# Attention matmuls of a fused attention and two-MLP kernel, planned as undivided blocks with the two array halves alternating

## The chip, the cores and the metric

The kernel runs on one core of a Trainium2 chip. The metric is device microseconds of one execution, and the time before is the median of three runs. A profiled execution, with its own time, gives the trace.

## What is computed

A block-recurrent attention with decay (2 batches, 8 heads, 768 positions, head size 64), whose output, transposed to 1536 tokens of width 512, goes through two MLPs, all in float32.

```python
def _attn_ref(q, k, v, lam):            # block = 64, nb = 12
    for b in range(nb):
        intra = np.einsum('bhic,bhjc->bhij', qb, kb) * Dmask[None]
        intra = np.einsum('bhij,bhjd->bhid', intra, vb)
        inter = np.einsum('bhid,bhde->bhie', qb * lam_pow[None], kv_state)
        out[:, :, sl] = intra + inter
        kv_state = lam_block[None, :, None, None] * kv_state + np.einsum('bhsd,bhse->bhde', kb_dec, vb)

def _moe_ref(x, w_gate, w_val, w_out):  # 512 -> 1536 -> 512
    return sigmoid(x @ w_gate) * (x @ w_val) @ w_out

def _moe2_ref(x, w_in, w_out):          # 512 -> 2048 -> 512
    return elu(x @ w_in) @ w_out
```

## The kernel before, in words

**Attention.** The 768 positions are taken in six chunks of 128 (the loop over `c`, line 562). For each chunk and each of the two batches `b` there are up to four sorts of TensorE work, each a group of small float32 matmuls: `st` (line 558), scores, eight per chunk and batch, four head pairs `p` times two halves `q`; its operands lie in 64 partitions, so it uses the upper or the lower half of the array's rows, and it writes one PSUM bank per half (`A1`, `B1`). `x` (line 595), scores times values, eight per chunk and batch, all 128 rows and 64 columns, where the column half is `q`. `x` again (line 600), state times query, from the second chunk on, 64 rows and 64 columns. `u` (line 579), the update of the state, sixteen per chunk, five chunks, 128 rows and 64 columns. In the trace each of these float32 matmuls is two MATMUL instructions, so eight matmuls are x16.

Between them stand VectorE's masking of the scores (`pr`, line 559), ScalarE's decayed keys (`kd`, line 569), GpSimd's decayed queries (`ql`, line 573), the state (`sn`) and `split_chunk` (line 420), which copies a finished chunk out of PSUM and splits it into a high and a low part for the MLPs.

**MLPs.** The products (`product`, line 451) are fp32r matmuls of 256 or 512 columns, three per term (high by high, high by low, low by high), on seven products a Strassen-like scheme; `unit` (line 650) does the output matmuls into `xu`. During the attention, the first MLP's products G and V for token part 0 follow chunk 1, for part 1 chunk 3 and for part 2 chunk 5 (lines 614 to 617). The name `warm` in the trace is PSUM bank A0: 24 bf16 matmuls at the start (line 543), and later the bank of the products.

**What sets the order.** The kernel's code only records operations (`Work.record`, line 160). `hazards` (line 179) works out what must precede what; `issue` (line 286) runs five rounds of a list scheduler (`run`, line 235), in which each engine takes, among its ready operations, the one with the highest priority from the backward run, and emits all instructions in the order of the best plan. Each engine then works in that order on the chip. The plan's times come from `cost` (line 135). A float32 matmul of n columns holds TensorE `n / 1.2 + 20` ns there, whatever stood before it. Every matmul is an operation of its own and may be planned anywhere between others. ScalarE's function tables (sigmoid, then exp) have an order among them (line 229) and no cost.

Of the kernel before, what the change touches and what calls it, by code (L numbers as in the profile page):

```python
# [3 lines left out]

# [1 line left out]

# [5 lines left out]
F32 = mybir.dt.float32  # L12
# [4 lines left out]
ALU = mybir.AluOpType  # L17
PSUM = bass.MemoryType.PSUM

P = 128  # L20
B, H, S, D = 2, 8, 768, 64
NP = H // 2
CH = 128
# [85 lines left out]


class Op:
    __slots__ = ("eng", "call", "reads", "writes", "gap", "took", "port", "table", "preds")


class Engine:
# [8 lines left out]

class Work:
    MATMUL = {512: (229, 391), 384: (173, 335), 256: (120, 283)}
    HANDOFF = {"tensor": 60, "vector": 35, "scalar": 35, "gpsimd": 78, "sync": 30}
    OVERLAP = {"vector": 83, "scalar": 101, "gpsimd": 45}

    def __init__(self, nc):  # L130
        self.nc, self.ops = nc, []
        for name in ENGINES:
            setattr(self, name, Engine(self, name))

    def cost(self, op, fn, args, kw):
        outs, ins = op.writes, [v for v in op.reads if v.ix.size > 1]
        n = (outs or op.reads)[0].ix.size
        on_chip = [v for v in ins if not v.buf.psum]
        op.port = False
        if op.eng == "tensor":  # L140
            dt = args[-1].dtype if len(args) > 2 else kw["rhs"].dtype
            if dt == F32R:
                return self.MATMUL[n]
            if dt == BF16:
                return n / 2.4 + 3, n / 2.4 + 170
            return n / 1.2 + 20, n / 0.6 + 210
        if op.eng == "sync":
            return 60, n * P * 4 / 400
        if op.eng == "gpsimd":
            op.port = len(on_chip) > 1  # L150
            took = 180 + 2.18 * n
        elif op.eng == "vector":
            single = len(ins) == 1 and len(on_chip) == 1 and not outs[0].buf.psum
            op.port = len(on_chip) > 1 or single
            took = 150 + 0.53 * n if single else 130 + 1.07 * n
        else:
            took = (190 if on_chip else 160) + 0.84 * n + (93 if len(op.reads) > 1 else 0)
        return took - self.OVERLAP[op.eng], took

    def record(self, eng, fn, args, kw):  # L160
        op = Op()
        op.eng = eng
        out, *rest = (kw[x] for x in ("out", *(x for x in kw if x != "out"))) if "out" in kw else (*args, *kw.values())
        op.writes = [out] if isinstance(out, View) else []
        op.reads = [v for v in rest if isinstance(v, View)]
        for v in op.reads + op.writes:
            assert v.turn >= v.buf.turn, "a tile is used behind its successor"
            v.buf.turn = v.turn
        op.gap, op.took = self.cost(op, fn, args, kw)
        func = kw.get("func", args[2] if fn == "activation" and len(args) > 2 else None)  # L170
        op.table = {AF.Sigmoid: 1, AF.Exp: 2}.get(func, 0)
        real = lambda v: v.ap() if isinstance(v, View) else v

        def call():
            return getattr(getattr(self.nc, eng), fn)(*(real(a) for a in args), **{k: real(a) for k, a in kw.items()})  # L175
        op.call = call
        self.ops.append(op)

    def hazards(self):
# [55 lines left out]
    def run(self, preds, key, backward=False):  # L235
        ops = self.ops[::-1] if backward else self.ops
        n = len(ops)
        after, left = [[] for _ in range(n)], [len(p) for p in preds]
        for k, p in enumerate(preds):
            for x in p:  # L240
                after[x].append(k)
        ripe, soon = {e: [] for e in ENGINES}, {e: [] for e in ENGINES}
        at, start, end = [0.0] * n, [0.0] * n, [0.0] * n
        free = dict.fromkeys(ENGINES, 0.0)
        port = queue = 0.0
        for k in range(n):
            if not left[k]:
                heapq.heappush(soon[ops[k].eng], (0.0, k))
        for _ in range(sum(op.eng is not None for op in ops)):
            t, e = min((free[e] if ripe[e] else max(free[e], soon[e][0][0]), i, e)  # L250
                       for i, e in enumerate(ENGINES) if ripe[e] or soon[e])[::2]
            while soon[e] and soon[e][0][0] <= t:
                k = heapq.heappop(soon[e])[1]
                heapq.heappush(ripe[e], (key[k], k))
            k = heapq.heappop(ripe[e])[1]
            op = ops[k]
            if e == "sync":
                queue = max(t + 1400, queue) + op.took
                free[e], end[k] = t + op.gap, queue + 300
            elif e == "tensor":  # L260
                t += 60 if t > free[e] + 1 else 0
                free[e], end[k] = t + op.gap, t + op.took
            else:
                go = max(t, port) if op.port else t
                if op.port:
                    port = go + op.gap
                free[e], end[k] = go + op.gap, go + op.took
            start[k] = t
            done = [k]
            while done:  # L270
                x = done.pop()
                for s in after[x]:
                    f = ops[s].eng
                    ready = free[e] if f == e == "tensor" and x == k else end[x] + self.HANDOFF.get(f, 0)
                    at[s] = max(at[s], ready)
                    left[s] -= 1
                    if left[s]:
                        continue
                    if f is None:
                        start[s] = end[s] = at[s]  # L280
                        done.append(s)
                    else:
                        heapq.heappush(soon[f], (at[s], s))
        return start, end
# [32 lines left out]
def tile_decay_attention_two_mlps(  # L317
# [13 lines left out]
    nc = work = Work(tc.nc)  # L331
    sb = Arena(ctx.enter_context(tc.tile_pool(name="sb", bufs=1)))
    ps = Arena(ctx.enter_context(tc.tile_pool(name="ps", bufs=1, space=PSUM)), psum=True)
# [202 lines left out]
    n = 1  # L536
# [14 lines left out]
    def scores(c):  # L551
        prs[c] = []
        for b in range(2):
            pr = sb.tile([P, 2, NP, CH], F32, f"woh_{b}", name="pr")
            for q, r in ((0, lo), (1, hi)):
                st = ps.tile([P, NP, CH], F32, ("A1", "B1")[q], name="st")
                for p in range(NP):
                    nc.tensor.matmul(st[:, p], lhsT=tin[c][r, b, 0, p], rhs=tin[c][r, b, 1, p], start=True, stop=True)
                nc.vector.tensor_tensor(out=pr[:, q], in0=st, in1=da[:, q], op=ALU.mult)
            prs[c].append(pr)  # L560

    for c in range(NCH):
# [10 lines left out]
                nc.gpsimd.tensor_tensor(out=ql[:, b], in0=tin[c][:, b, 1], in1=lp, op=ALU.mult)  # L573
        if more:
            u = ps.tile([P, 2, NP, D], F32, "C1", name="u")
            for b in range(2):
                for p in range(NP):
                    for q, r in ((0, lo), (1, hi)):
                        nc.tensor.matmul(u[r, b, p], lhsT=kd[:, b, 2 * p + q], rhs=nat_of[c][:, b, 1, 2 * p + q],
                                         start=True, stop=True)  # L580
            sn = sns[c + 1] = sb.tile([P, 2, NP, D], F32, f"wt1_{c % 2}", name="sn")
            if c == 0:
                nc.vector.tensor_copy(sn, u)
            else:
                for p in range(NP):
                    nc.vector.scalar_tensor_tensor(out=sn[:, :, p], in0=sns[c][:, :, p], scalar=l_ch[:, p],
                                                   in1=u[:, :, p], op0=ALU.mult, op1=ALU.add)
        xa = sb.tile([P, 6, CH], F32, "wol_1", name="xa")
        later = []
        parts = None  # L590
        for b in range(2):
            x = ps.tile([P, NP, CH], F32, f"xu_{b}", name="x")
            for p in range(NP):
                for q, r in ((0, lo), (1, hi)):
                    nc.tensor.matmul(x[r, p], lhsT=nat_of[c][:, b, 1, 2 * p + q], rhs=prs[c][b][:, q, p],
                                     start=p == 0 or not c, stop=not c, skip_group_check=True)
            if c:
                for p in range(NP):
                    for r in (lo, hi):
                        nc.tensor.matmul(x[r, p], lhsT=sns[c][r, b, p], rhs=ql[r, b, p], start=False, stop=True,  # L600
                                         skip_group_check=True)
            if b == 0:
                parts = split_chunk(xops[s], slice(t0, t0 + CH), x, later, xa)
            else:
                later.append(x)
            next(parts)
# [211 lines left out]
```

## Time and profile before

| what | value |
|---|---|
| median of three runs | 621.32 us (620.34 to 622.68) |
| the profiled execution, its own time | 623.05 us |
| its span, first to last instruction | 621.3 us |
| mean granted TensorE clock | 0.999 |
| TensorE (PE) busy | 609.7 us, 98% |
| VectorE (DVE) / ScalarE (ACT) / GpSimd (POOL) busy | 398.7 / 301.1 / 327.0 us |

The profile counts an instruction as busy from its start to its modelled end. TensorE's matmuls overlap, so what one costs is read from its start to the next one's start.

### The profile page before, as it was taken

Reading aid. Unit: us, or ns where it says so; the run is one execution under the profiler, and the core shown is the slowest. Engines: PE = TensorE matmul, PEld = TensorE weight load, DVE = VectorE, ACT = ScalarE, POOL = GpSimd, SP = SyncE. Lnnn points to the kernel's source line nnn. Section 1 sums busy time; section 2 is a strip of 40 time slices with the busy share of each in tenths; the row PEclk is TensorE's granted clock in tenths of the full one; section 3 lists DMA queues with packets and bytes.
Section 4 is the critical chain, followed back from the end, with each engine's and each line's share of the span. In section 5 each row is a group of like instructions: output and inputs, shape, how many; then the busy total and the mean of one; then the engine's idle time right before and its main releaser. Section 6 shows DMA issues by size and latency. Waiting matters only on the chain.

```text
span 621.3 us, 9271 instructions
## 1 busy us (share of the span) xinstructions
PE 609.7 (98%) x3632; PEld 516.3 (83%) x3632; DVE 398.7 (64%) x684; ACT 301.1 (48%) x571; POOL 327.0 (53%) x264
## 2 busy tenths in 40 slices
PE   9999999999899999999999899999999999999997
PEld 5778888988788888888899788888788888888886
DVE  5657646536855755755755988485757776776474
ACT  3655234665324425424414788783728282844160
POOL 2458435858747737737624897447546364551100
PEclk9999999999999999999999999999999999999999
DMA  8913110233032111111110110311311211200005
GB/s 323 418 74 136 69 69 7 77 122 134 8 130 69 69 68 69 69 68 69 69 68 2 69 69 0 136 70 68 137 68 69 69 69 69 68 1 1 0 18 186
DMA packets 8828, 51.98 MB, mean 84 GB/s; under 512 B 1104, under 2 KB 1360, under 8 KB 3024
## 3 DMA queue, kind: packets, MB, share of 16 engines
q1 hardware_dynamic: 8784, 51.39, 22.3%
q8 instruction: 28, 0.46, 0.3%
q14 instruction: 16, 0.13, 0.1%
HBM read 48.24 MB, written 3.15 MB: 83 GB/s over the span
## 4 chain that ended last, share of the span: by engine, by line
PE 85%; DVE 5%; ACT 4%; DMA 3%; issue 2%; POOL 2%; ACTq 0%; SPq 0%; DVEq 0%; POOLq 0%
PE xu L175 32%; PE B L175 17%; PE warm L175 10%; PE A L175 9%; PE C L175 6%; PE x L175 5%; PE st L175 4%; DVE w L175 2%; DMA w<-in_w_in 2%; ACT w L175 1%; PE u L175 1%; DMA w<-in_w_gate 1%; POOL t L175 1%; ACT gh L175 1%; DVE xu L175 0%
## 5 line engine op out<-in xcount | busy, mean ns | idle before, releaser
L175 PE MATMUL xu<-gh,woh 128*128 128x512 f32 (+1 forms) x322 | 126.5, 396 | 4.9 <-DVE acc L175 2.5
L175 PE MATMUL xu<-gl,woh 128*128 128x512 f32 (+1 forms) x322 | 125.3, 390 | 0.0
L175 PE MATMUL xu<-gh,wol 128*128 128x512 f32 (+1 forms) x322 | 124.9, 389 | 0.0
L175 DVE TENSOR_TENSOR acc<-xu,acc 128x512 f32<-128x512 f32 x120 | 81.5, 688 | 49.6 <-PE xu L175 49.0
L175 POOL TENSOR_TENSOR gl<-sig,gh 128x1024 fp32r<-128x1024 f32 (+1 forms) x38 | 81.4, 2154 | 44.3 <-ACT gh L175 43.3
L175 POOL TENSOR_TENSOR t<-w 128x256 f32<-128x256 f32 (+1 forms) x80 | 69.0, 891 | 49.1 <-DVE w L175 45.0
L175 POOL TENSOR_TENSOR l<-t,h 128x768 fp32r<-128x768 f32 (+1 forms) x38 | 64.1, 1692 | 35.2 <-ACT h L175 32.6
L175 PEld LDWEIGHTS xu<-gh,woh 128*128 128x128 f32 x322 | 60.5, 188 | 19.6 <-issue 3.4
L175 PEld LDWEIGHTS xu<-gh,wol 128*128 128x128 f32 x322 | 60.5, 188 | 12.1
L175 PEld LDWEIGHTS xu<-gl,woh 128*128 128x128 f32 x322 | 60.6, 188 | 10.0
L175 POOL TENSOR_TENSOR wol<-w,woh 128x512 fp32r<-128x512 f32 x26 | 33.2, 1294 | 63.7 <-ACT woh L175 57.4
L175 ACT CAST gh<-sig 128x512 fp32r<-128x512 f32 (+1 forms) x58 | 45.0, 784 | 25.0 <-DVE sig L175 22.9
L175 ACT ACTIVATE w<-w 128x1024 f32<-128x1024 f32 x34 | 38.7, 1137 | 29.3 <-POOL wol L175 14.9
L175 DVE SCALAR_TENSOR_TENSOR w<-w,w 128x1024 uint32<-128x1024 uint32 x34 | 50.6, 1489 | 0.2
L175 DVE TENSOR_SCALAR w<-w 128x1024 uint32<-128x1024 uint32 x34 | 35.0, 1030 | 24.1 <-ACT w L175 23.8
L175 ACT ACTIVATE sig<-B 128x256 f32<-128x256 f32 (+1 forms) x62 | 28.4, 458 | 38.3 <-PE B L175 34.0
L175 DVE TENSOR_TENSOR wt<-B,wt 128x256 f32<-128x256 f32 (+1 forms) x45 | 22.9, 508 | 28.9 <-PE B L175 26.0
L175 ACT CAST h<-t 128x512 fp32r<-128x512 f32 (+1 forms) x40 | 29.1, 727 | 14.9 <-POOL t L175 8.4
L175 ACT ACTIVATE sig<-sig 128x256 f32<-128x256 f32 (+1 forms) x68 | 34.2, 507 | 1.4
L175 ACT ACTIVATE sig<-warm 128x256 f32<-128x256 f32 x36 | 13.8, 383 | 40.9 <-PE warm L175 21.8
L175 ACT CAST woh<-w 128x1024 fp32r<-128x1024 f32 x14 | 14.8, 1054 | 38.5 <-PE xu L175 27.8
L175 POOL TENSOR_TENSOR ql<-tin,low 128x512 f32<-128x512 f32 x10 | 13.5, 1362 | 35.1 <-PE x L175 22.4
(143 smaller groups left out, 1558.0 us busy)
## 6 DMA issues: line engine op xcount, KB each, us to landing
w<-in_w_out SPq DMA_DIRECT2D x14, 1024.0 KB, 4.8
w<-in_w_in SPq DMA_DIRECT2D x8, 1024.0 KB, 4.8
nat<-in_att SPq DMA_DIRECT2D x6, 1024.0 KB, 10.1
w<-in_w_gate SPq DMA_DIRECT2D x6, 1024.0 KB, 4.9
w<-in_w_val SPq DMA_DIRECT2D x6, 1024.0 KB, 4.8
tin<-in_att SPq DMA_DIRECT2D x5, 1024.0 KB, 10.5
out_t<-o SPq DMA_DIRECT2D x11, 256.0 KB, 2.0
tin<-in_att SPq DMA_DIRECT2D x2, 512.0 KB, 6.2
```

What stands on the lines that cost most here:

```text
L175: return getattr(getattr(self.nc, eng), fn)(*(real(a) for a in args), **{k: real(a) for k, a in kw.items()})
```

## The change

Every run of attention matmuls that belongs together (one `st`, one `u`, one of each kind of `x`) is recorded inside `with nc.together()`, which joins them into one operation of the plan, never divided, whose reads and writes are those of all its parts. In `scores` the loop order changes: per head pair first the lower, then the upper half, into both banks, then the two VectorE multiplications. The plan's cost of a float32 matmul becomes `n / 2.4 + 2.5` ns held and `n / 1.2 + 165` ns to its end. TensorE operations get a `shape`, and the plan adds 150 ns where the shape differs from that of the operation before. The plan adds 1283 ns where ScalarE's table changes. No instruction's operands, size or number changes, nor do buffers or DMAs.

```diff
+    SWITCH, TABLE = 150, 1283
...
         if op.eng == "tensor":
-            dt = args[-1].dtype if len(args) > 2 else kw["rhs"].dtype
+            dt = kw["rhs"].dtype
+            op.shape = dt if dt != F32 else (kw["lhsT"].halves, kw["lhsT"].ix.size) if len(kw["rhs"].halves) < 2 else kw["lhsT"].ix.size
...
-            return n / 1.2 + 20, n / 0.6 + 210
+            return n / 2.4 + 2.5, n / 1.2 + 165
...
+    @contextmanager
+    def together(self):
+        self.block = []
+        yield
+        parts, self.block = self.block, None
+        op = parts[0]
+        calls = [x.call for x in parts]
+        op.took = sum(x.gap for x in parts) + parts[-1].took - parts[-1].gap
+        op.gap = sum(x.gap for x in parts)
+        op.reads = [v for x in parts for v in x.reads]
+        op.writes = [v for x in parts for v in x.writes]
+        op.call = lambda: [c() for c in calls][-1]
         self.ops.append(op)
...
             elif e == "tensor":
                 t += 60 if t > free[e] + 1 else 0
+                t += self.SWITCH if op.shape != shape else 0
+                shape = op.shape
                 free[e], end[k] = t + op.gap, t + op.took
             else:
+                if op.table and op.table != table:
+                    t, table = t + self.TABLE, op.table
...
-            for q, r in ((0, lo), (1, hi)):
-                st = ps.tile([P, NP, CH], F32, ("A1", "B1")[q], name="st")
+            sts = [ps.tile([P, NP, CH], F32, bank, name="st") for bank in ("A1", "B1")]
+            with nc.together():
                 for p in range(NP):
-                    nc.tensor.matmul(st[:, p], lhsT=tin[c][r, b, 0, p], rhs=tin[c][r, b, 1, p], start=True, stop=True)
-                nc.vector.tensor_tensor(out=pr[:, q], in0=st, in1=da[:, q], op=ALU.mult)
+                    for st, r in zip(sts, (lo, hi)):
+                        nc.tensor.matmul(st[:, p], lhsT=tin[c][r, b, 0, p], rhs=tin[c][r, b, 1, p], start=True, stop=True)
+            for q in range(2):
+                nc.vector.tensor_tensor(out=pr[:, q], in0=sts[q], in1=da[:, q], op=ALU.mult)
...
+            with nc.together():
+                for b in range(2):
+                    for p in range(NP):
+                        for q, r in ((0, lo), (1, hi)):
+                            nc.tensor.matmul(u[r, b, p], lhsT=kd[:, b, 2 * p + q],
+                                             rhs=nat_of[c][:, b, 1, 2 * p + q], start=True, stop=True)
...
```

The two groups of `x` (lines 593 and 598) get the same `with` around their loops, whose order stays (head pair, then half).

## Rows read from the trace of the kernel before

**Rows 1.** The page: busy time, and the chain that ended last by engine.
```profile
PE 609.7 (98%) x3632; PEld 516.3 (83%) x3632; DVE 398.7 (64%) x684; ACT 301.1 (48%) x571; POOL 327.0 (53%) x264
...
PE 85%; DVE 5%; ACT 4%; DMA 3%; issue 2%; POOL 2%; ACTq 0%; SPq 0%; DVEq 0%; POOLq 0%
```

**Rows 2.** Busy time of each engine by stretch (us, instructions), clock, DMA share, GB/s.
```profile
10.00:20.00 10.00, 9.96 (x116) 8.09 (x113) 7.03 (x13) 6.62 (x18) 4.60 (x4) 1.00 1.02 424
...
30.00:40.00 10.00, 10.00 (x89) 8.05 (x85) 7.48 (x15) 6.94 (x16) 7.50 (x5) 1.00 0.38 156
...
6.00:29.00 23.00, 22.96 (x238) 17.68 (x237) 12.93 (x25) 11.78 (x33) 9.31 (x8) 1.00 1.02 422
29.00:100.00 71.00, 71.00 (x648) 58.58 (x646) 42.03 (x87) 29.82 (x68) 34.06 (x25) 1.00 0.23 88
100.00:182.00 82.00, 79.02 (x444) 68.38 (x443) 50.23 (x71) 39.70 (x69) 58.32 (x50) 1.00 0.24 90
...
340.00:400.00 60.00, 56.82 (x334) 49.62 (x333) 47.71 (x104) 48.63 (x107) 45.09 (x37) 1.00 0.15 54
```

**Rows 3.** Waits from 6 to 100 us: engine waiting, for whom, us, times, longest.
```profile
ACT xa L175 <- PE x L175: 27.5, 8, 9.2
POOL ql L175 <- PE x L175: 22.4, 3, 8.1
DVE pr L175 <- PE st L175: 14.5, 11, 3.4
```

**Rows 4.** TensorE's groups from 6.1 to 99.6 us: count, busy us, mean ns, idle.
```profile
L175 PE MATMUL st<-tin 64*128 64x128 f32 x192 | 26.3, 288 | 0.0
L175 PE MATMUL x<-pr,nat 128*64 128x128 f32 x192 | 21.3, 282 | 0.0
L175 PE MATMUL x<-ql,sn 64*64 64x128 f32 x160 | 15.8, 278 | 0.0
L175 PE MATMUL u<-nat,kd 128*64 128x64 f32 x160 | 9.3, 228 | 0.0
...
L175 PE MATMUL warm<-x11h,h 128*128 128x256 f32 x8 | 2.6, 322 | 0.0
```

**Rows 5.** TensorE in order of time, last chunk: start us, us, group, count.
```profile
92.35 1.09 PE L175 MATMUL x<-pr,nat 128*64 128x128 f32 x8
93.36 1.16 PE L175 MATMUL st<-tin 64*128 64x128 f32 x8
94.45 1.08 PE L175 MATMUL x<-ql,sn 64*64 64x128 f32 x8
95.46 1.09 PE L175 MATMUL x<-pr,nat 128*64 128x128 f32 x8
96.48 1.08 PE L175 MATMUL x<-ql,sn 64*64 64x128 f32 x8
97.50 1.09 PE L175 MATMUL x<-pr,nat 128*64 128x128 f32 x16
98.52 1.09 PE L175 MATMUL x<-ql,sn 64*64 64x128 f32 x16
99.54 0.39 PE L175 MATMUL B<-xPh,h 128*128 128x256 f32 x1
...
99.88 0.28 PE L175 MATMUL B<-xPh,l 128*128 128x256 f32 x1
100.00 0.28 PE L175 MATMUL B<-xPh,h 128*128 128x256 f32 x1
```

**Rows 6.** TensorE in order of time, elsewhere in the attention.
```profile
6.04 1.71 PE L175 MATMUL st<-tin 64*128 64x128 f32 x16
7.68 1.90 PE L175 MATMUL warm<-idle 128*128 128x512 bf16 x8
...
29.11 1.71 PE L175 MATMUL st<-tin 64*128 64x128 f32 x16
...
49.35 1.15 PE L175 MATMUL u<-nat,kd 128*64 128x64 f32 x32
50.44 1.16 PE L175 MATMUL st<-tin 64*128 64x128 f32 x8
...
63.75 0.28 PE L175 MATMUL warm<-xPl,h 128*128 128x256 f32 x1
63.96 0.87 PE L175 MATMUL x<-pr,nat 128*64 128x128 f32 x6
...
60.36 0.38 PE L175 MATMUL warm<-x143h,l 128*128 128x256 f32 x1
60.68 0.65 PE L175 MATMUL x<-ql,sn 64*64 64x128 f32 x4
```

**Rows 7.** ScalarE: the decayed keys of chunk 1 in time, and the table loads.
```profile
18.25 3.32 ACT L175 ACTIVATE kd<-nat,low 128x128 f32<-128x128 f32 x11
...
L175 ACT ACT_TABLE_LOAD x3 | 3.8, 1283 | 0.8 <-PEq L806 0.8
```

More of the change, by code (lines that the diff above doesn't have):

```diff
@@ L2 @@
 import re
-from contextlib import ExitStack
+from contextlib import ExitStack, contextmanager
 import numpy as np
@@ L111 @@
 class Op:
-    __slots__ = ("eng", "call", "reads", "writes", "gap", "took", "port", "table", "preds")
+    __slots__ = ("eng", "call", "reads", "writes", "gap", "took", "port", "table", "preds", "shape")
 class Engine:
@@ L130, in __init__ @@
     def __init__(self, nc):
-        self.nc, self.ops = nc, []
+        self.nc, self.ops, self.block = nc, [], None
         for name in ENGINES:
@@ L176, in record @@
         op.call = call
+        if self.block is None:
+            self.ops.append(op)
+        else:
+            self.block.append(op)
+    @contextmanager
[10 more added lines that the diff above has]
+        op.call = lambda: [c() for c in calls][-1]
         self.ops.append(op)
@@ L245, in run @@
         port = queue = 0.0
+        shape = table = None
         for k in range(n):
@@ L575, in tile_decay_attention_two_mlps @@
             u = ps.tile([P, 2, NP, D], F32, "C1", name="u")
[L576 to L580, printed above, removed]
+            with nc.together():
[4 more added lines that the diff above has]
+                                             rhs=nat_of[c][:, b, 1, 2 * p + q], start=True, stop=True)
             sn = sns[c + 1] = sb.tile([P, 2, NP, D], F32, f"wt1_{c % 2}", name="sn")
@@ L592, in tile_decay_attention_two_mlps @@
             x = ps.tile([P, NP, CH], F32, f"xu_{b}", name="x")
[L593 to L596, printed above, removed]
-            if c:
[L598 to L601, printed above, removed]
+            with nc.together():
+                for p in range(NP):
+                    for q, r in ((0, lo), (1, hi)):
+                        nc.tensor.matmul(x[r, p], lhsT=nat_of[c][:, b, 1, 2 * p + q], rhs=prs[c][b][:, q, p],
+                                         start=p == 0 or not c, stop=not c, skip_group_check=True)
+            if c:
+                with nc.together():
+                    for p in range(NP):
+                        for r in (lo, hi):
+                            nc.tensor.matmul(x[r, p], lhsT=sns[c][r, b, p], rhs=ql[r, b, p], start=False, stop=True,
+                                             skip_group_check=True)
             if b == 0:
```

## The prediction

> **What bounds the kernel now.** First the page: TensorE (PE) is busy 98% of the span, and the chain that ended last is 85% PE [rows 1]. That is a mean over stages, so the stretches come next: from 6 to 29 us and from 29 to 100 us PE has no idle time worth the name, while VectorE (DVE) is busy 42 of 71 us in the second [rows 2]. The waits of that time say the same from the other side: the long ones are ScalarE, GpSimd and DVE waiting for PE's `x` and `st` [rows 3]. So in the attention PE ends last. The order of time then shows what a busy PE does there. Eight `x` instructions of one half take 1.01 us to the next start (92.35 to 93.36), and sixteen with alternating halves take 1.02 us (97.50 to 98.52); for the other `x` it is 1.02 us for eight (94.45 to 95.46) and 1.02 for sixteen (98.52 to 99.54) [rows 5]. The second half of the array is free of charge if it is asked for in turn. `st` of one half takes 1.09 us for eight (93.36 to 94.45) [rows 5]; sixteen with the lower half ahead of the upper take 1.64 us (6.04 to 7.68), so they overlap only in part [rows 6]. A change of shape costs besides: a product, normally 0.12 us to the next start (99.88 to 100.00) [rows 5], takes 0.21 us (63.75 to 63.96) or 0.32 us (60.36 to 60.68) ahead of an attention matmul [rows 6].
>
> **What the change takes from PE.** It removes no instruction and adds none; it puts them in another order. The attention lasts from 6.04 us [rows 6] to 99.54 us [rows 5], 93.5 us. In it lie products of 256 columns, the groups of eight of which one stands in [rows 4]: 21 groups, 163 matmuls, 163 x 0.12 = 19.6 us. Thirteen bf16 matmuls of the start fill 13/8 x 1.90 = 3.1 us [rows 6]. The rest, 70.8 us, is attention with its changes of shape.
>
> After the change every group is a block. The counts of [rows 4] make 192/16 = 12 blocks `st`, 12 `x` of the scores, 160/16 = 10 `x` of the state and 160/32 = 5 `u`. An alternating `st` is not in the trace; by the two `x`, where sixteen cost what eight do, it takes the 1.09 us of eight (bounds: 1.02, as `x`, and 1.64, as now). So 12 x 1.09 + 12 x 1.02 + 10 x 1.02 + 5 x 1.09 (`u`, 49.35 to 50.44 [rows 6]) = 41.0 us. A block behind a product adds 0.09 to 0.20 us, 0.145 in the mean; if all 39 do, 5.7 us. PE's work in the attention falls from 70.8 to at most 46.7 us, by 24 us.
>
> One rule speaks against a third of that. The page "TensorE: Matmul & The Clock Gate" of the Trainium skill says, in the part on packing small matmuls, that a weight load overlaps a running matmul only when the row group differs. By it the column halves of the first `x` and of `u`, which use all rows, would gain nothing from taking turns. The trace differs: the sixteen at 97.50 us are of just this kind.
>
> **What of it reaches the end.** Two stages, because different things can take PE's place.
>
> Chunks 0 and 1, up to 29.11 us, where chunk 2's `st` starts [rows 6]. DMA is saturated here (share 1.02 at 422 GB/s [rows 2]), and the decayed keys of chunk 1 start only at 18.25 us [rows 7]. Behind that lie at least one `u` and four `x` blocks, 1.09 + 4 x 1.02 = 5.2 us, so chunk 1 can't end before 23.4 us: a gain of 0 to 5.7 us. I take 4, nearer the upper end, since PE is busy 22.96 of 23 us here [rows 2] and is not waiting for the data as it is.
>
> Chunks 2 to 5, 29.11 to 99.54 us, 70.4 us. PE's need falls to 8 x 1.09 + 16 x 1.02 + 3 x 1.09 = 28.3 us, plus 27 x 0.145 = 3.9, plus the products' 19.6: 51.8 us, a gain of 18.6. But DVE keeps its 42.0 us of work [rows 2]; it would have to be busy 81% of the time. The fullest stretches in the trace with the attention's mix are 70% (10 to 20 us) and 75% (30 to 40 us) [rows 2]. Work that runs in a fixed order with handoffs will hardly do better, so I take 75%: 42.0 / 0.75 = 56 us, a gain of 14.4 us. Bounds: 51.8 us (PE still sets the pace, 18.6) and 42.0 / 0.70 = 60 us (10.4).
>
> The rest of the kernel keeps its instructions. Their order comes from a plan with other costs, so small waits can move. PE is idle 3.0 us from 100 to 182 us and 3.2 us from 340 to 400 us [rows 2], where the weights' preparation and the handover to the second MLP end last: I take 0 and keep 3 us either way for the range. The first of these stages starts when the attention ends, and its weights wait for buffers that the attention frees, so it moves forward as a whole. The table cost moves nothing by itself: there are three loads of 1.28 us [rows 7], and the order among the functions that makes it three is kept.
>
> Edits with no price of their own: both `st` halves now wait for both banks, and the two multiplications stand together; what covers that is another block or the products, 19.6 us of them. If that cover is missing, the wait is a DVE operation or two per block, which is the slower rival below. The planned cost of eight small matmuls is now 8 x 55.8 = 0.45 us where the trace shows 1.02. The old figure, 8 x 126.7 = 1.01, was right for an alternating block and too small for the fragments that the old plan made of them. With 150 ns per change of shape the new plan undercounts the attention about as the old one did, so I give it no cost and no gain.
>
> **The sum.** 4 + 14.4 = 18.4 us. The profiled execution took 623.05 us by its own time with a span of 621.3 us; it would come to 604.7 with a span of 602.9. The median of the runs shown, 621.32, lies 1.7 us under that time, so the median after is forecast at 603 us.
>
> **The rivals.**
> PE stays the bound all through: DVE runs at 81%, the first stage gives all it can. For it speaks that DVE's waits in the attention are waits for PE [rows 3] and vanish with them; against it, that no stretch is so full. Gain 5.7 + 18.6 = 24.3, time 597 us, 593 to 599 with the small waits.
> Other engines take half: DVE runs at 70%, data keep the first stage at 29 us. Gain 10.4, time 611 us, 607 to 616.
> Column halves don't take turns: a block of the first `x` takes 2.04 us, two times eight, instead of 1.02. Then PE needs 8 x 1.02 = 8.2 us more in the second stage, 60 us, and about 4 more in the first: gain 10.4, time 611 us. This is what the rule above would make of it. The sixteen in 1.02 us [rows 5] speak against it almost alone and enough.
> The change doesn't do what it says, because what is freed turns into waits at PE almost wholly: 616 to 624 us. Against it: products stand ready in most of this time.
> Slower: a block is never divided, and PE works in order. If each block stands at PE's head until its last operand (the second `pr`, the later bank) is there, and nothing else can pass, PE waits per block. 24 us over 39 blocks is 0.62 us; from that wait on the change is slower, and with two DVE operations of 0.7 us per block, 39 x 1.4 = 55 us, less the cover of the products 19.6, less the gain 24, it would be 11 us slower, 632 us. Against it: the plan knows all operands of a block and fills ahead of it, and only the `st` and first `x` blocks have such a partner.
>
> **How the numbers follow.** Forecast, 598 to 607 us: 0.47. PE stays the bound: 0.20. Other engines take half: 0.20. No turns: 0.02. Nothing gained: 0.06. Slower: 0.05. The range, 594 to 614, takes in the first four but for their outer ends (0.07) and leaves out the last two, 0.18 in all. A measurement of this kernel can tell about 0.5%, 3.1 us: faster than 618.2 is the first four and a little of the fifth, 0.90; within, 0.05; slower than 624.4, 0.05.
>
> **What would show it.** Right: in the profile after, sixteen `st` instructions in one piece of about 1.1 us to the next start, no pieces of `x` with two or four; the last attention block ends near 81 us; DVE is busiest of the helpers in 29 to 80 us, near 75%; PE shows several us of idle time there that it had not; the stages behind last as long as before. Wrong in the size of the blocks, if `st` stays over 1.3 us. Wrong in the second stage, if PE has no idle time there (597) or over 8 us (611). The forecast as a whole is wrong if the attention still ends past 90 us, or if the stages from 100 us on grow by more than 3 us.

## The result and the profile after

The changed kernel takes 610.88 us (median of 4 runs, 609.63 to 612.5); beside it the kernel before takes 620.92 (4 runs). The ratio is 0.9835, interval 0.9804 to 0.9866: faster by 10.0 us where 18.4 were forecast. The profiled execution took 610.83 us by its own time, with a span of 609.1; the one before was itself 2.1 us over its median, so the two traces differ by 12.2 us of span and the medians by 10. One execution of e3, the profiled one, ran in a slower state of the chip (mean clock 0.983); its time and its trace are left out below.

The page of after; [rows 1] has the same two lines of before.

```profile
PE 589.6 (97%) x3631; PEld 501.4 (82%) x3632; DVE 401.6 (66%) x684; ACT 301.5 (49%) x571; POOL 324.8 (53%) x264
...
PE 84%; DVE 6%; ACT 4%; issue 3%; DMA 2%; POOL 2%; ACTq 0%; DVEq 0%; SPq 0%; POOLq 0%
```

The chain is PE's as before (84% for 85), so nothing else has become the bound of the whole. But PE's busy time fell by 20.1 us and the span by 12.2 only: PE now has idle time that it did not have. TensorE in order of time shows that the blocks are what they should be (columns as in [rows 5]):

```profile
68.09 1.09 PE L177 MATMUL x<-ql,sn 64*64 64x128 f32 x16
69.11 0.39 PE L177 MATMUL B<-xPh,h 128*128 128x256 f32 x1
...
70.02 1.16 PE L177 MATMUL st<-tin 64*128 64x128 f32 x16
71.11 0.39 PE L177 MATMUL C<-x143h,h 128*128 128x256 f32 x1
...
76.90 1.09 PE L177 MATMUL x<-pr,nat 128*64 128x128 f32 x16
77.92 1.09 PE L177 MATMUL x<-ql,sn 64*64 64x128 f32 x16
...
80.99 0.38 PE L177 MATMUL B<-xPh,h 128*128 128x256 f32 x1
```

From start to next start: `st` 1.09 us, both sorts of `x` 1.02. In the whole trace the attention stands in 37 pieces (10 of `st`, 12 and 10 of `x`, 5 of `u`), where before it stood in 99. It ends at 80.99 us; before it ended at 99.54 [rows 5]. That is 18.5 us of lead, and 18.4 was the sum of the prediction.

The lead is lost later. To follow it, PE's product work was added up in both traces (0.12 us for 256 columns, 0.227 for 512) and the time at which each mark is reached was compared:

| product work done, us | 40 | 100 | 280 | 300 | 440 | 460 | 520 |
|---|---|---|---|---|---|---|---|
| reached before, us | 120.8 | 184.6 | 370.3 | 390.4 | 533.6 | 553.9 | 614.4 |
| reached after, us | 102.0 | 164.0 | 349.5 | 376.6 | 519.1 | 541.6 | 602.1 |
| lead, us | 18.7 | 20.7 | 20.8 | 13.8 | 14.5 | 12.3 | 12.2 |

It grows by 2 us (a PE wait of 2.5 us for `acc`, which the kernel before has near 165 us, is gone), is steady for 180 us, and then falls by 7.0 us between 349.5 and 376.6 us, the handover to the second MLP, and by 2.2 near 534. PE's longest waits of after, in total, times, longest:

```profile
PE B L177 <- DVE x22l L177: 3.6, 1, 3.6
PE st L177 <- DVE pr L177: 3.3, 3, 2.1
...
PE xu L177 <- DVE acc L177: 2.0, 2, 1.8
```

**The 7 us.** The first of these waits lies in the handover. The three engines there, in order of time, first VectorE:

```profile
352.19 4.85 DVE L177 TENSOR_TENSOR gl<-sig,gh 128x512 fp32r<-128x512 f32 x1
356.96 0.69 DVE L177 TENSOR_TENSOR xu<-xu,acc 128x512 f32<-128x512 f32 x1
357.56 0.41 DVE L177 TENSOR_TENSOR x22l<-xu,x22h 128x256 fp32r<-128x256 f32 x1
```

GpSimd:

```profile
350.64 1.86 POOL L177 TENSOR_TENSOR l<-t,h 128x768 fp32r<-128x768 f32 x1
352.46 1.44 POOL L177 TENSOR_TENSOR xPl<-xt,xPh 128x256 fp32r<-128x256 f32 x2
353.86 1.41 POOL L177 TENSOR_TENSOR l<-w,h 128x256 fp32r<-128x256 f32 x2
355.24 1.25 POOL L177 TENSOR_TENSOR l<-t,h 128x512 fp32r<-128x512 f32 x1
```

TensorE:

```profile
358.03 0.58 PE L177 MATMUL B<-x22l,h 128*128 128x256 f32 x1 [3.57 <-DVE x22l L177]
...
361.44 0.63 PE L177 MATMUL xu<-gh,woh 128*128 128x512 f32 x1
361.87 0.63 PE L177 MATMUL C<-x143h,h 128*128 128x512 f32 x1
```

One VectorE operation, `gl`, takes 4.85 us; before, one of this shape took 0.72 (at 370.93 us). When it starts, GpSimd has an operation in flight (until 352.50), five more follow without a gap, and `gl` ends 0.55 us after the last of them (356.49). Behind `gl` stands `x22l`, for which PE waits 3.6 us. When PE goes on, a 512-column product takes 0.43 us to the next start where 0.23 is usual: the windows show the clock.

```profile
340.00:400.00 60.00, 55.38 (x294) 47.30 (x293) 44.59 (x82) 45.18 (x97) 36.18 (x34) 0.94 0.16 58
...
355.00:360.00 5.00, 1.65 (x5) 1.27 (x6) 5.00 (x10) 2.24 (x6) 1.58 (x3) 0.74 0.00 0
360.00:365.00 5.00, 5.00 (x19) 4.19 (x18) 4.54 (x8) 2.25 (x4) 4.73 (x3) 0.58 0.00 0
```

The mean of 0.58 is 4.2 us at the lower level (1.2 GHz) and 0.8 at the higher. From 358.03 to 364.2 us PE works at half speed and so loses 3.1 us; with the waits of 3.57 and 0.32 that is the 7.0 of the table. (Between the same marks PE had no idle time before: 20.1 us busy of 20.1.) The 2.2 us near 534 are the same pair of engines:

```profile
530.56 4.95 DVE L177 TENSOR_SCALAR w<-w 128x1024 uint32<-128x1024 uint32 x1 [0.21 <-ACT w L177]
```

```profile
530.19 4.76 POOL L177 TENSOR_TENSOR gl<-sig,gh 128x1024 fp32r<-128x1024 f32 x2
```

Nor is it new. The wait near 165 us in the kernel before stands behind such an operation too:

```profile
161.51 5.18 DVE L175 TENSOR_SCALAR w<-w 128x1024 uint32<-128x1024 uint32 x1 [0.24 <-ACT w L175]
```

Such a meeting does not always end so. This is the one that cost the kernel before its 2.5 us, as it came out in the changed kernel, VectorE and then GpSimd:

```profile
143.05 2.87 DVE L177 TENSOR_SCALAR w<-w 128x1024 uint32<-128x1024 uint32 x1 [0.23 <-ACT w L177]
```

```profile
142.95 5.23 POOL L177 TENSOR_TENSOR gl<-sig,gh 128x1024 fp32r<-128x1024 f32 x2
```

Here `w` got in after the first of the two GpSimd operations (2.87 us for 5.18), and the second waited for it (5.23 us for the pair, 4.70 before). So by these rows the 2 us that the lead gains near 165 us are an outcome of this kind rather than the blocks' doing; what decides between the two outcomes is not shown.

On the engines' access to SBUF, the page "SBUF — State Buffer" of the Trainium skill (Who interferes with whom) says that VectorE and GpSimd share a port pair as an exclusive lock, and that who comes second is blocked for the whole instruction of the other. The lock agrees with these rows. That the block lasts for one instruction agrees with the 2.87 us at 143.05, but not with the handover, where `gl` waited out the rest of one instruction and five more. That the ports are the place where the two meet is the page's word; the runs show only that VectorE is long when GpSimd runs beside it.

**The attention's own idle time.** The same windows as in [rows 2], cut at the new end:

```profile
6.00:29.00 23.00, 18.84 (x267) 14.40 (x268) 16.80 (x32) 13.71 (x38) 12.85 (x10) 1.00 1.01 420
29.00:80.00 51.00, 49.27 (x604) 43.47 (x600) 37.36 (x77) 27.74 (x62) 32.60 (x23) 0.97 0.31 123
...
24.48:80.99 56.51, 52.61 (x647) 46.25 (x643) 42.52 (x89) 31.20 (x72) 36.80 (x27) 0.97 0.36 145
```

DVE is 73% busy in the second (37.36 of 51). The third line is the prediction's second stage, from chunk 2's `st` to the end of the attention: DVE is busy for 42.5 of 56.5 us, the 75% assumed. But in the first stage, where PE had no idle time, it is now idle for 4.2 of 23 us. The longest wait of it, TensorE and then VectorE:

```profile
23.39 1.15 PE L177 MATMUL u<-nat,kd 128*64 128x64 f32 x32
24.48 1.16 PE L177 MATMUL st<-tin 64*128 64x128 f32 x16
27.70 1.75 PE L177 MATMUL st<-tin 64*128 64x128 f32 x16 [2.06 <-DVE pr L177]
```

```profile
24.59 1.12 DVE L177 SCALAR_TENSOR_TENSOR sn<-sn,low,u 128x128 f32<-128x128 f32 x4 [1.34 <-PE u L177]
25.63 0.42 DVE L177 TENSOR_TENSOR x11l<-x,x11h 128x256 fp32r<-128x256 f32 x1
25.97 0.75 DVE L177 TENSOR_TENSOR sums<-x,xa 128x256 f32<-128x256 f32 x2
26.63 0.41 DVE L177 TENSOR_TENSOR x22l<-x,x22h 128x256 fp32r<-128x256 f32 x1
26.96 1.28 DVE L177 TENSOR_TENSOR pr<-st,low 128x512 f32<-128x512 f32 x2
```

Two `st` blocks stand back to back, and the second needs the banks of the first, which `pr` empties only after four groups of other VectorE work. That is the mechanism of the slower rival, in three places (3.3 us in all) and not in 39.

### The profile page after: what moved, and what is told of

The parts are those of the page before. It is cut to its first block, busy times and chain, and to the rows that moved or that the text cites. A ratio compares the mean times of both kernels' runs of the same rounds, so it can differ in the third digit from the quotient of the medians.

```text
span 609.1 us, 9285 instructions
## 1 busy us (share of the span) xinstructions
PE 589.6 (97%) x3631; PEld 501.4 (82%) x3632; DVE 401.6 (66%) x684; ACT 301.5 (49%) x571; POOL 324.8 (53%) x264
## 4 chain that ended last, share of the span: by engine, by line
PE 84%; DVE 6%; ACT 4%; issue 3%; DMA 2%; POOL 2%; ACTq 0%; DVEq 0%; SPq 0%; POOLq 0%
PE xu L177 35%; PE B L177 18%; PE A L177 10%; PE warm L177 10%; PE C L177 6%; PE x L177 3%; DVE w L177 2%; PE st L177 2%; DVE sums L177 1%; DMA w<-in_w_gate 1%; ACT w L177 1%; PE u L177 1%; POOL t L177 1%; DMA w<-in_w_in 1%; ACT gh L177 1%
## 5 line engine op out<-in xcount | busy, mean ns | idle before, releaser
L177 PE MATMUL xu<-gh,woh 128*128 128x512 f32 (+1 forms) x322 | 127.8, 400 | 4.5 <-DVE xt L177 2.4
L177 POOL TENSOR_TENSOR gl<-sig,gh 128x1024 fp32r<-128x1024 f32 (+1 forms) x38 | 79.9, 2118 | 45.4 <-ACT gh L177 44.6
L177 PE MATMUL B<-x22l,h 128*128 128x256 f32 (+1 forms) x90 | 29.2, 325 | 3.6 <-DVE x22l L177 3.6
L177 POOL TENSOR_TENSOR l<-w,h 128x256 fp32r<-128x256 f32 x36 | 26.2, 740 | 7.7 <-ACT h L177 7.7
## 6 DMA issues: line engine op xcount, KB each, us to landing
nat<-in_att SPq DMA_DIRECT2D x6, 1024.0 KB, 12.8
```

## The experiments

Two questions. First, the handover: my theory is that the table cost changed the plan so that VectorE's `gl` met GpSimd's gap-free run, and that the shared access to SBUF made it long; the rival is that the loss lies in the new blocks or in the order as such. Second, the attention: my theory became that planning a block at half its real time is not free; the rival, the prediction's own step, is that it costs nothing. Before each batch the kernel before took 620.13, 620.26 and 620.31 us (7 runs each).

**One wait added (e1).** The order of every engine stays; GpSimd's next operation with shared access waits for VectorE's `gl` where the plan has put `gl` first.

```diff
-                        port = made
-                    elif False:
+                        port = made if op.writes[0].buf.name in ("gl0", "gl1") else None
+                    elif op.eng == "gpsimd" and port is not None:
```

> The changed kernel with the same order of instructions on every engine; only GpSimd's next operation waits for VectorE's low part of g (gl) where the plan put that one ahead. Theory (port): of the lead of 18.6 us that the attention gives, 7 us are lost from 349 to 377 us, because one gl on VectorE takes 4.85 us instead of 0.7 while GpSimd's operations follow one another without a gap; TensorE then waits 3.6 us for x22l and runs at half its clock for some 5 us. With the wait that gl takes under 2 us, TensorE's longest wait in that stage is under 1.5 us, the granted clock from 355 to 365 us is 1.0 (0.58 to 0.74 in the changed kernel), and the time is 603 to 606 us. Rival (order): the wait comes from the plan's order in the handover itself; GpSimd's operations, moved back, delay the next operands by as much, and the time stays at 609 to 612 us.

Measured: 604.35 us (603.27 to 605.91), ratio 0.9749, 0.9728 to 0.977, 6.5 us under the changed kernel. VectorE, GpSimd and the windows of the handover:

```profile
354.77 0.88 DVE L177 TENSOR_TENSOR gl<-sig,gh 128x512 fp32r<-128x512 f32 x1
```

```profile
355.73 1.44 POOL L177 TENSOR_TENSOR xPl<-xt,xPh 128x256 fp32r<-128x256 f32 x2 [0.63 <-DVE gl L177]
```

```profile
355.00:360.00 5.00, 4.70 (x30) 4.00 (x29) 5.00 (x13) 4.82 (x13) 4.20 (x6) 1.00 0.00 0
360.00:365.00 5.00, 5.00 (x33) 4.37 (x32) 5.00 (x8) 2.89 (x8) 4.48 (x3) 1.00 0.00 0
```

`gl` takes 0.88 us, PE's wait is gone and the clock stays at 2.4 GHz. The meeting with GpSimd is shown to be the cause of the long `gl`, and the long `gl` that of the lost clock.

The 6.5 us are not the one wait's alone. By the marks of the table above, e1 takes 21.2 us from 280 to 300 (27.1 in the changed kernel, 20.1 before), so the wait gives back 5.9 us. From 440 to 460 it takes 20.3 (22.5 and 20.3): near 530 us no wait was added, `w` again started 0.37 us behind GpSimd's `gl`, and this time it got in after the first and took 2.59 us. Against that, the attention ended at 83.42 us, 2.4 later than in the changed kernel, with the same order.

**No table cost (e2), and then the wait too (e6).**

```diff
-    SWITCH, TABLE = 150, 1283
+    SWITCH, TABLE = 150, 0
```

> The changed kernel with the function table's cost in the plan at zero; blocks, turns and the cost of a change of shape stay. Theory (port): the loss in the handover hangs on how VectorE's and GpSimd's operations happen to lie, not on the table; the attention still ends at 79 to 84 us, and the handover (340 to 400 us) loses anything between 0 and 7 us: 604 to 612 us. Rival (table): counting the table moved the exp ahead and caused the loss; without it the stage loses no more than in the kernel before, and the time is 603 to 605 us.

Measured: 605.46 us (603.51 to 607.14), ratio 0.9764, 0.9738 to 0.979, 5.4 us under the changed kernel. No `gl` of 4 us is left in the handover; near 148 us the wait of before is back, 2.5 us behind a VectorE operation of 5.15. The time lies in the theory's range and almost in the rival's, so it does not part them, and it is a net figure: the attention ends at 83.65 us, 2.7 later than in the changed kernel, and the meeting near 148 us came out long.

The profiles together say more. In all with the table's cost in the plan and no added wait (the changed kernel, e4, e12) one `gl` of the handover takes 4.85 to 4.89 us; in all without that cost (the kernel before, e2, e5, e8 to e11) none takes over 1.8. So the table edit, which moves no instruction by itself, decided the order in which `gl` met GpSimd.

> No cost for the table, and GpSimd waits for VectorE's gl where the plan put that ahead; the order on every engine is that of the run without the table's cost. Theory (port): that plan has no gl over 3 us in the handover, so the wait has little left to mend: 602 to 606 us, at most 2 us under the run without the table's cost. Rival (the wait helps anywhere): 598 to 601 us.

Measured: 606.63 us (604.54 to 608.89), 0.6 above the range and 1.2 over e2, within the scatter of both. With no long `gl` left to prevent, e1's wait brings nothing more, as the theory of shared access has it.

**GpSimd waits for every VectorE operation with shared access (e7).** As e1, with `port = made` kept and only the `elif False` replaced.

> The changed kernel with GpSimd waiting for each VectorE operation that the plan puts ahead and that needs the shared way to SBUF, not only gl; the order on every engine stays. Theory (port): the 4.95 us of VectorE's w at 530 us goes too (2 us), and in the attention the w and l of 1.9 to 2.1 us get shorter; but GpSimd is now held by VectorE all through the kernel: 601 to 607 us. Rival (held): GpSimd, over 90% busy in several stretches, falls behind; the time is 608 us or more, with TensorE waiting for what GpSimd makes.

Measured: 608.22 us (607.04 to 608.43), 2.7 under the changed kernel and 3.9 over e1. Holding GpSimd everywhere gives back more than half of what the one wait brings. The time is the rival's, but PE's waits for GpSimd come to 0.6 us only, so its mechanism is not shown. The `w` near 530 us takes 2.62 us, as in e1, which had no wait there.

**The costs without the blocks (e4).** `together` records the parts one by one, and `scores` is that of before; the new costs stay.

> The changed kernel's plan costs (small matmuls, change of shape, table) with neither blocks nor alternating halves: the matmuls are recorded as before, one operation each. Theory: the fragments of two and four stay and st gets no turns; the attention ends at 92 to 101 us and the time is 613 to 624 us. Rival (the counted changes of shape gather the matmuls by themselves): st still without turns, but few fragments of x; the attention ends near 87 us.

Measured: 626.84 us (622.82 to 631.1), ratio 1.0111, 1.0054 to 1.0168: slower than before and over the 613 to 624 expected. The attention ends at 101.28 us, and the handover has the same wait for `x22l` (3.6 us) behind a `gl` of 4.88. All of the gain is the blocks' and turns'; the new costs alone take 6.7 us, and in the profile 6.9 are lost in the handover (27.0 us from mark 280 to 300 for 20.1).

**The blocks with the old costs (e5).**

```diff
-    SWITCH, TABLE = 150, 1283
+    SWITCH, TABLE = 0, 0
...
-            return n / 2.4 + 2.5, n / 1.2 + 165
+            return n / 1.2 + 20, n / 0.6 + 210
```

> The changed kernel's blocks and alternating halves with the plan's old costs: 126.7 ns per small matmul, nothing for a change of shape or table. Theory: what TensorE saves comes from the blocks and turns alone, and the old 126.7 ns is near the 1.02 us that a block takes; the attention ends at 80 to 86 us and, as the handover to the second MLP is then planned as in the kernel before, the time is 602 to 607 us. Rival (counting): without the counted changes of shape the blocks stand among products more often, and the attention ends past 88 us, the time is over 610 us.

Measured: 598.1 us (597.63 to 598.51), ratio 0.9641, 0.9627 to 0.9656. That is 12.8 us under the changed kernel and better than expected; the attention ends at 77.05 us. So the second question is decided against my step. Three further runs divide the 12.8 us among the three costs.

**One cost at a time: e10 (only the halved matmul cost), e11 (old cost, 150 ns per change of shape), e12 (old cost, the table cost).** The blocks are in all three.

> Blocks and turns with the changed kernel's n / 2.4 + 2.5 ns per small matmul alone; nothing for a change of shape, nothing for the table. Theory (undercount): a block is taken for 0.45 us, less still; the attention ends at 81 to 87 us, the time is 603 to 610 us. Rival (counted changes of shape spoil the order): without them the time is that of the old costs, 597 to 600 us.

> Blocks and turns with the old n / 1.2 + 20 ns per small matmul and 150 ns per change of shape; no cost for the table. Theory (undercount): a block is taken for 1.16 us, a little too long, which harms less than too short: the attention ends at 76 to 80 us, the time is 597 to 602 us. Rival (counted changes of shape spoil the order): 603 to 607 us.

> Blocks and turns with the old n / 1.2 + 20 ns per small matmul, nothing for a change of shape, but 1283 ns for a change of the table. Theory (table, by way of the port): the attention ends at 76 to 79 us as with the old costs alone, and the handover to the second MLP loses 4 to 7 us more than there, with one VectorE operation of over 4 us in it; the time is 602 to 606 us. Rival (the table's cost does no harm when the rest is right): 597 to 600 us.

Measured against e5's 598.1: e10 605.34 us (602.51 to 609.39), 7.2 more; e11 599.31 (597.27 to 600.63), 1.2 more, within the scatter; e12 602.89 (597.79 to 605.48), 4.8 more in the median. e12 spreads over 7.7 us, from e5's time to well over it; its profile is of the execution at 605.48 and has the long `gl`, VectorE and then TensorE:

```profile
348.79 4.89 DVE L177 TENSOR_TENSOR gl<-sig,gh 128x512 fp32r<-128x512 f32 x1
```

```profile
354.66 0.39 PE L177 MATMUL B<-x22l,h 128*128 128x256 f32 x1 [3.63 <-DVE x22l L177]
```

The execution at 597.79 was not profiled; that `gl` escapes there is likely and not shown. The profiles of e10 and e5 lie 4.9 us apart, of which 4.6 are there when the attention ends (81.62 and 77.05); both are of the fastest execution of their run, and no trace shows the rest of the 7.2. The attention's windows of e10 show where the half cost goes: PE is idle 3.4 and 3.0 us in them (1.5 and 0.3 in e5), and the clock in the first is 0.93 (1.00 in e5).

```profile
6.00:29.00 23.00, 19.63 (x257) 15.21 (x257) 16.34 (x30) 12.91 (x37) 11.81 (x10) 0.93 1.01 421
29.00:80.00 51.00, 47.98 (x598) 42.11 (x600) 36.64 (x80) 28.00 (x64) 31.27 (x23) 1.00 0.32 122
```

PE's longest waits in this time, in total, times, longest:

```profile
PE st L177 <- DVE pr L177: 2.1, 2, 1.4
PE warm L177 <- DVE l L177: 1.9, 2, 1.2
PE warm L177 <- ACT h L177: 1.2, 2, 0.7
```

In e5 `st` waits 0.7 us for `pr`, and the products (`warm`) wait for neither `l` nor `h`.

**Measured costs (e9).** A block planned at what the trace shows, 0.87 + 0.15 = 1.02 us, and no table cost.

```diff
-    SWITCH, TABLE = 150, 1283
+    SWITCH, TABLE = 150, 0
...
-            return n / 2.4 + 2.5, n / 1.2 + 165
+            return n / 1.2 + 2.5, n / 1.2 + 165
```

> Blocks and turns with the plan's cost at what the trace shows: n / 1.2 + 2.5 ns per small matmul, so 0.87 us for eight, and 150 ns per change of shape, together 1.02 us as measured; no cost for the table. Theory (undercount): the run without the table's cost (605.5 us) lost against the run with the old costs (598.1 us) because its plan takes a block for 0.45 + 0.15 = 0.60 us and so sets the other engines' order for a TensorE that is faster than it is; with the measured cost the attention ends at 76 to 80 us and the time is 597 to 601 us. Rival (counted changes of shape spoil the order): as the 150 ns stay, the time stays at 604 to 607 us.

Measured: 595.17 us (594.76 to 595.66), ratio 0.9592, 0.9577 to 0.9606: under the 597 to 601 expected, and the best version: 15.7 us under the changed kernel and 25.1 under the kernel before. Its windows and TensorE's time around the second `st`:

```profile
6.00:29.00 23.00, 22.29 (x315) 17.61 (x314) 17.62 (x37) 15.90 (x43) 11.90 (x10) 1.00 1.01 421
23.67:75.35 51.68, 51.60 (x645) 45.36 (x643) 39.65 (x85) 29.82 (x68) 35.93 (x27) 1.00 0.43 164
340.00:400.00 60.00, 59.76 (x333) 51.53 (x332) 41.88 (x83) 46.29 (x98) 40.43 (x35) 1.00 0.20 71
```

```profile
23.67 1.16 PE L177 MATMUL st<-tin 64*128 64x128 f32 x16
24.76 1.15 PE L177 MATMUL u<-nat,kd 128*64 128x64 f32 x32
25.84 0.39 PE L177 MATMUL warm<-x11h,h 128*128 128x256 f32 x1
...
27.60 1.43 PE L177 MATMUL st<-tin 64*128 64x128 f32 x16
```

`u` and twelve products, 1.8 us of them, fill the time in which `pr` empties the banks; the second `st` starts at the same time as in the changed kernel, and PE has done that work meanwhile. The attention ends at 75.35 us, and the handover has no wait over 1.1 us.

**No turns: e3, the changed kernel with `st` as two blocks of one half each; e8, the same without the table cost.**

```diff
-            sts = [ps.tile([P, NP, CH], F32, bank, name="st") for bank in ("A1", "B1")]
-            with nc.together():
-                for p in range(NP):
-                    for st, r in zip(sts, (lo, hi)):
+            for q, r in ((0, lo), (1, hi)):
+                st = ps.tile([P, NP, CH], F32, ("A1", "B1")[q], name="st")
+                with nc.together():
+                    for p in range(NP):
...
```

> The changed kernel with each st as two blocks of one half each, lower then upper, instead of one with the halves alternating. Theory: a block of one half takes 1.09 us as the alternating one of both does, so TensorE has up to 12 x 1.09 = 13 us more to do until the attention ends; about half of it fell on time that TensorE now spends waiting, so the attention ends at 86 to 92 us instead of 81, and the time is 615 to 622 us if the handover loses the same 7 us. Rival (blocks alone): the gain comes from fewer changes of shape, and the attention ends at 80 to 84 us.

Measured: 611.77 us (median of three, 609.66 to 614.77), under the 615 to 622 expected; it is 0.9 over the changed kernel, and the two spreads overlap. So e3 decides nothing on the turns.

> No cost for the table, and each st as two blocks of one half each. To be read against the run without the table's cost (605.5 us, attention until 83.7 us). Theory: the twelve further blocks of 1.09 us are 13 us of TensorE's work, of which a third to two thirds fall on time in which it waits now; the attention ends at 88 to 93 us, the time is 610 to 615 us. Rival (blocks alone): under 607 us.

Measured: 611.61 us (608.63 to 616.35), 6.2 over e2, with the attention's end at 89.08 us instead of 83.65. Without turns `st` needs 12 x 1.09 = 13 us more of PE; about 5 to 6 of them reach the end. The rest of the gain goes with the blocks; how much the turns bring with costs that fit a block (e9) was not tried.

## Why the prediction was right and wrong

**Right: the sizes.** `st` takes 1.09 us, `x` 1.02; the column halves do take turns, as [rows 5] had it. The rule weighed there, of the Trainium skill's page "TensorE: Matmul & The Clock Gate" (packing small matmuls), would, as the prediction read it, have made the `x` at 76.90 us last 2.04. The rule is about weight loads; the step from there to whole column halves was the prediction's own.

**Right: that other work takes PE's place.** Chunk 2's `st` starts at 24.48 us for 29.11 [rows 6], a gain of 4.6 where I took 4; from there to the end of the attention it is 56.5 us, with DVE at 75%, where I took 56. The end, "near 81 us", came at 80.99.

**Wrong: "I give it no cost and no gain".** The halved matmul cost takes 7.2 us in the medians (e10 beside e5) and 4.9 in the profiles, and it was hidden in a sum that came out right: with costs that are true of a block the attention ends at 75.35 to 77.05 us and the lead is 22.5 to 24.2, which is the rival "PE stays the bound" (24.3). So DVE's 75% was not the limit that I took it for, although the changed kernel showed just this figure. In e9 chunks 2 to 5 take 51.7 us (23.67 to 75.35), which is the bound of 51.8, and PE is idle for 0.1 us of it. DVE is 77% busy there and need not reach 81%, because 39.65 us of its work lie in this stage where I took 42.0. The step compared 0.45 us with the fragments' undercount of before and called the two alike. But before, nothing had to wait for a whole block; now a block that is planned too short can stand at PE's head before its banks are free. That is one part only: of e10's 6.4 us of idle time in the attention, 2.1 are of this kind, 3.1 are products waiting for operands that VectorE and ScalarE had not made yet, and the lower clock comes on top. Each setting of the costs gives one order, so some of this could be the luck of an order; but the four runs that plan a block of eight at 1.01 to 1.16 us (e5, e9, e11, e12) end the attention at 75.35 to 78.33 us, and the three that plan it at 0.45 to 0.60 (the changed kernel, e2, e10) at 80.99 to 83.65. e11 is a warning against reading the first stage alone: PE is busy there for 19.58 of 23 us, no more than in e10, and e11 is 6 us faster.

**Wrong: "The table cost moves nothing by itself" and "I take 0" for the rest of the kernel.** It changed the plan's order, and VectorE's `gl` came to stand against GpSimd's run. That costs 7.0 us in the handover of the changed kernel's profile, of which e1 gives back 5.9; in the medians the cost is 5.4 us (changed kernel beside e2) and 4.8 (e12 beside e5). I allowed 3 us either way. The other 2.2 us of the stages behind the attention went in the meeting near 530 us, which e1 shows can also end well. The sign was there to be read: VectorE's 5.18 us at 161.51 us in the trace before.

**The sum.** Blocks in turn with the old costs -22.2 us (e5), the halved cost +7.2, the table cost +5.4 by e2: -9.6, and -10.0 was measured. The two prices are taken from different bases and need not add up so well.

**The time and the signs.** 610.88 us is inside the range of 594 to 614, but above the forecast's own 598 to 607 and in the band of "Other engines take half" (607 to 616), whose conditions did not come: DVE stood at 75%, not 70%, and chunk 2 began at 24.48 us, not 29. The sum for the attention came out; the step that failed is "I take 0" behind it. By the prediction's own sign (the stages from 100 us on grow by more than 3 us) the forecast as a whole is wrong: they grew by 8.5, the lead's fall from 20.7 to 12.2.

**Not the cause:** blocks waiting at PE's head all through (slower by 11 us in that rival). e5 and e9 have the same blocks and hardly a wait of this kind.

**Left open.** With the same order the attention ended at 80.99 us in the changed kernel, 83.42 in e1 and 83.03 in e7. In e1 two `x` blocks at 18.91 and 20.68 us took 1.77 and 1.89 us where those at 18.69 and 19.72 in the changed kernel took 1.03 and 1.02. The granted clock from 6 to 29 and from 29 to 80 us is 0.93 and 0.93 in e1, 0.92 and 0.94 in e7, 1.00 and 0.97 in the changed kernel; by these shares the lower clock takes about 3.5 us more in both (an estimate), which covers the difference. Why PE's clock fell in the one and not in the other was not tried.

## What to carry to other kernels

Put into a planner what a trace shows for the unit that it plans: here one constant, half of the measured time, and one small penalty took back more than half of what the blocks gave (22 us to 10). When a stage gets shorter, look in the stages behind it for a VectorE operation that may come to stand beside a gap-free run of GpSimd operations, and put it first with a wait on GpSimd at that one place; a wait at every such operation gave most of the gain back. A forecast sum that comes out right can hide two errors, so test the terms.

## What was unexpected of the hardware

A VectorE operation of 0.7 us took 4.85 to 5.18 us beside back-to-back GpSimd work, in the kernel before, in the changed one, in e2, e4 and e12. In the changed kernel both ended 0.55 us after GpSimd's run did (357.04 after 356.49, 535.51 after 534.95); with GpSimd made to wait it took 0.88. The same pair of operations can also take turns: `w` took 2.87 us at 143.05 in the changed kernel and 2.59 near 530 us in e1.

A PE wait of 3.6 us cost about as much again in clock: 6.2 us of work at 1.2 GHz after it. After the waits of the first stage the clock is lower too, although PE is busy all the time (changed kernel; e9 has 1.00 in the same stretch):

```profile
31.00:36.00 5.00, 5.00 (x64) 4.51 (x63) 1.84 (x4) 1.68 (x5) 2.36 (x2) 0.79 0.59 236
```
